# Gate, up and down products of a GEGLU feed-forward with fp32 operands in column tiles of 32, instead of three products of split operands

## The chip, the cores and the metric

The kernel runs on one core of a Trainium2 chip. The core has TensorE for matrix products (PE in the profile, its weight loads PEld), VectorE (DVE), ScalarE (ACT), GpSimd (POOL) and SyncE (SP), which issues the DMAs here. Matrix products read SBUF and write PSUM, of which the kernel uses eight banks of 128 partitions by 512 fp32 numbers. The metric is the device time of one execution in microseconds, the median over runs.

A matmul takes a stationary operand, the weights, loaded by an instruction of its own, and streams a moving operand past it. Both operands of the kernel are fp32 numbers in memory. A product can be asked for in `fp32r`, a reduced form, or in `fp32`.

## The reference

One transformer block on 2048 tokens of width 576 (D), 32 heads of 18, a feed-forward of width 4608 (F), everything in fp32:

```python
xn = _layernorm(x, axis=-1)
s = _A_ref(xn, A_wqkv, A_wo)          # softmax attention over all 2048 keys
g = _silu(_B_ref(xn, B_w_gate, B_w_up, B_w_down))
return x + s * g
# _B_ref: (gelu(x @ w_gate) * (x @ w_up)) @ w_down
```

Gelu is the tanh form.

## The kernel before

Tokens are taken in four blocks of 512 (`TB`). The kernel has four stretches.

- *Projections* (pool `pro`). For each block: layer norm, transposition of the normalized tokens by TensorE (`transposes`), a copy to SBUF with a split into a high and a low part by `split_t` (ScalarE copies into an fp32r tile, VectorE subtracts), queries and keys (`project`), values (`values_of`). The transposed tokens go to DRAM as two parts (`store_xt`, tensor `xhs`), from where `load_xd` brings them back for the feed-forward, with a GpSimd copy into the other half of the partitions.
- *Lead* (ten sections): feed-forward sections, the later ones with the maxima of the first scores between their products.
- *Attention* (128 sections): each holds a feed-forward section and a quarter of the attention of four heads over one token block.
- *Epilogue* (six sections): the rest of the feed-forward with the output projection.

A *section* (function `section`) makes one hidden tile of 128 of the 4608 hidden columns for one block: 4 blocks x 36 tiles = 144 sections. The contraction over D = 576 goes in nine chunks of 64 rows. The gate weights lie in partitions 0 to 63 and the up weights in 64 to 127, and so do two copies of the tokens, so that `gate_up` runs a gate product `pg` and an up product `pu` side by side in the two row halves of the array. Each chunk has three terms: high weights by high tokens, low by high, high by low. That is 27 pairs of matmuls of 64 x 128 weights by 512 tokens, all fp32r. The weights come by `load_gu`, one section ahead, and are split by GpSimd in `split_gu` (L106 the high part, L108 the low one).

Between these pairs stand the *specials* of the section: in the attention stretch 16 pairs, each a score product `pe` (L729) in one row half and a product `pm` for the running maximum of later scores (L698) in the other, both 64 x 128 and fp32r. `spread` deals them out evenly. ScalarE turns `pe` into exponentials (L730), VectorE reduces `pm` (L699). Every second section also multiplies exponentials by values (`acc`, L764): an unsplit fp32 product with 128 rows and 32 weight columns for each of four heads, the four in the four column groups of the array.

`activate` makes the hidden tile: Square on ScalarE (L426), VectorE (L427), tanh (L437), then VectorE once more (L440); up times gate is taken out of PSUM before that (L431, L434). `finish` splits the result into `hh` and `hl` (L106, L108) and the down weights into `dh` and `dl`.

Two hidden tiles make a *down* round (`G = 2`): eight sums of 128 tokens by 288 columns, each of 2 tiles x 3 terms, added to `Y` by VectorE (L453). In the attention stretch `half_downs` makes them with 64 rows at a time, one row half working on one sum while the other works on another, held apart by marks on ScalarE (L470). Nine of the 72 rounds are made by `down` with all 128 rows. A round's products stand behind the gate and up products of the section after its second tile.

TensorE takes its instructions in the order of the program (`manual_schedule`); the order on the other engines comes from the framework's scheduler, with some instructions kept in program order (`kept`, `no_sync`). SP issues all DMAs in one order. Tags `f`, `m` and `s` name the PSUM banks: 2, 3 and 3.

Of the kernel before, what the change touches and what calls it, by code (L numbers as in the profile page):

```python
# [17 lines left out]
P = 128  # L18
# [29 lines left out]
BANKS = {"f": 2, "m": 3, "s": 3}  # L48
EPS = 1e-5
# [20 lines left out]
def kernel(ctx: ExitStack, tc: tile.TileContext, x, wqkv, wo, w_gate, w_up, w_down, out):  # L70
# [19 lines left out]
    xhs = [dram.tile([2, D, TB], F32, name=f"xhs{b}") for b in range(NB)]  # L90
# [28 lines left out]
    def raw_tile(shape, pool=wts):  # L119
        return pool.tile(shape, F32, name="raw", tag="raw", bufs=2)  # L120

    def load_gu(t, keep=lambda i: i):

        raw = raw_tile([P, NC, P])
        for a, w in enumerate((w_gate, w_up)):
            keep(nc.sync.dma_start(raw[HR * a:HR * a + HR], w[:, t * P:(t + 1) * P].rearrange("(k p) n -> p k n", p=HR)))
        return raw, [], []

    def split_gu(w, k, keep=lambda i: i):
        hi, lo = (wts.tile([P, XG, P], F32R, name=m, bufs=5) for m in ("wh", "wl"))  # L130
        first = split(hi, lo, w[0][:, XG * k:XG * k + XG, :], keep)
        w[1].append(hi)
        w[2].append(lo)
        return first

    def load_xd(b, key=None):

        xd = [[], []]
        for c in range(0, NC, XG):
            for i in range(2):  # L140
                t = wts.tile([P, XG, TB], F32R, name=f"xd{i}_{c}")
                asked[:] = [nc.sync.dma_start(f(t)[0:HR], xhs[b][i, c * HR:(c + XG) * HR, :]
                                              .rearrange("(k p) t -> p k t", p=HR))]
                if key:
                    no_sync(asked[0], key, "keys first")
                copied[:] = [nc.gpsimd.tensor_copy(t[HR:P], t[0:HR])]
                xd[i].append(t)
        return xd
# [8 lines left out]
    with tc.tile_pool(name="pro", bufs=1) as pro, tc.tile_pool(name="pps", bufs=1, space=PSUM) as pps:  # L157
# [27 lines left out]
        def split_t(pt, k, xt):  # L185

            if k < KT:
                nc.scalar.activation(xt[0][:, k, :], pt, AF.Copy)
# [45 lines left out]
        def transposes(b, xr):  # L234
            xt = XT[b % 2]
            pts = [pps.tile([P, TB], F32, name="pt", bufs=KT + 1) for k in range(KT + 1)]
            for j in range(4):
                if b == 0 and j == 0:
                    warm(46)
                for k in range(KT + 1):  # L240
                    nc.tensor.transpose(pts[k][:, j * P:(j + 1) * P], xr[j][:, k * P:(k + 1) * P], ident)  # L241
            for k in range(KT + 1):
                split_t(pts[k], k, xt)
            return xt

        def store_xt(b, xt):
            keep = tc.keep_in_program_order if b == 0 else lambda i: i
            for i in range(2):
                keep(nc.sync.dma_start(xhs[b][i, 0:R0, :].rearrange("(k p) t -> p k t", p=P), f(xt[i])))
                keep(nc.sync.dma_start(xhs[b][i, R0:D, :], f(xt[2])[HR * i:HR * i + HR, :]))  # L250
# [96 lines left out]
        for b in range(NB):  # L347
# [29 lines left out]
            if b == 2:  # L377
                ahead = load_gu(0, tc.keep_in_program_order)
                for k in range(NG):
                    split_gu(ahead, k)  # L380
# [22 lines left out]
    def gate_up(tag):  # L403

        w, xd = FF["w"], FF["xd"]
        pg, pu = (ps.tile([P, TB], F32, name=n, tag=tag, bufs=BANKS[tag]) for n in ("pg", "pu"))
        terms = [(wp, *divmod(c, XG), xp) for c in range(NC) for wp, xp in ((0, 0), (1, 0), (0, 1))]

        def pair(i):
            wp, k, c, xp = terms[i]  # L410
            for a, o in enumerate((pg, pu)):
                rr = slice(HR * a, HR * a + HR)
                nc.tensor.matmul(o, w[1 + wp][k][rr, c, :], xd[xp][k][rr, c, :], start=(i == 0),  # L413
                                 stop=(i == len(terms) - 1))

        return [lambda i=i: pair(i) for i in range(len(terms))], pg, pu
# [6 lines left out]
    def activate(pg, pu, early):  # L423

        t1 = ffn.tile([P, TB], F32, name="t1", bufs=2)
# [10 lines left out]
        def rest(behind=None, evicted=None):  # L436
            tanh = kept(nc.scalar.activation(t1, t1, AF.Tanh, scale=GC * GS))  # L437
            if behind:
                no_sync(tanh, behind, "a mark first")
            one = kept(nc.vector.scalar_tensor_tensor(t1, t1, 1.0, t2 if early else pg, op0=ALU.add, op1=ALU.mult))  # L440
# [17 lines left out]
    DOWN = [(a, w, g) for g in range(G) for a, w in ((0, 0), (0, 1), (1, 0))]  # L458
# [4 lines left out]
    def down_product(py, hs, wd, j, c, i, rr=slice(0, P), start=False, stop=False):  # L463
        a, w, g = DOWN[i]
        return nc.tensor.matmul(py, hs[g][a][rr, j * P:(j + 1) * P], wd[w][rr, g, 288 * c:288 * c + 288],  # L465
                                start=start, stop=stop)
# [7 lines left out]
    def half_downs(b, r, hs, wd, Y):  # L474
# [9 lines left out]
        def downs_of(a, ks):  # L484
            for k in ks:
                for i in range(m):
                    def step(k=k, i=i):
# [6 lines left out]
                        one = down_product(pys[k], hs, wd, j, c, i, slice(HR * a, HR * a + HR), fresh,  # L494
                                           begun == 0 and i == m - 1)
                        if begun == 0 and i == 0 and k in seen:
                            after(one, seen[k])
# [31 lines left out]
    def load_down(r, raw):  # L529
        kept(nc.sync.dma_start(raw, w_down[r * G * P:(r + 1) * G * P, :].rearrange("(g p) n -> p g n", p=P)))  # L530
        return raw

    def section(specials=(), tag="f", raw_d=None, ahead=True):
# [17 lines left out]
        if nxt:  # L551
            for k in range(NG - 1 if ahead else 0):
                first = split_gu(nxt, k, kept)
                if k == 0 and n in ATT and n > ATT.start:
                    no_sync(first, FF["hl"], "hidden values first")
        if g == G - 1:
            FF["rawd"] = load_down(r, raw_d() if raw_d else raw_tile([P, G, D])) if ahead else FF.pop("next_d")
        for p in spread(pairs, specials):
            p()
        if nxt and ahead:  # L560
            split_gu(nxt, NG - 1, kept)
# [15 lines left out]
    def finish(pool=ffn, cut=split, bufs=1):  # L577

        n = FF["n"] - 1
        b, r = divmod(n // G, NR)  # L580
        hh = ffn.tile([P, TB], F32R, name="hh", bufs=G + 1)
        hl = ffn.tile([P, TB], F32R, name="hl", bufs=G + 1)
        first = cut(hh, hl, FF["act"])
        if n in ATT and copied:
            no_sync(first, copied.pop(), "transposed x first")
        FF["hl"] = low_part[0]
        FF["hs"].append((hh, hl))
        if n % G == G - 1:
            wd = [pool.tile([P, G, D], F32R, name=m, bufs=bufs) for m in ("dh", "dl")]
            cut(*wd, FF["rawd"])  # L590
            for h in range(2):
                once = n in ATT and n + G in ATT
                FF["down"].append((b, r, FF["hs"], wd, FF["Y"], (2 * h, 2 * h + 1), once, n + 1 + (0 if once else h)))
# [51 lines left out]
    with tc.tile_pool(name="att", bufs=1, reuse_waits="tile") as att:  # L645
# [155 lines left out]
        def lead_raw():  # L801
            t = att.tile([P, QD, TB], F32, name="pT", bufs=8)
            return t.rearrange("p a t -> p (a t)")[:, 0:G * D].rearrange("p (g d) -> p g d", g=G)

# [7 lines left out]
        for n, m in enumerate(FIRST):  # L812
            none = [lambda: None]
            lead = [lambda s=s: lead_pair(s) for s in range(slot, slot + m)]
            section((n == 2) * 5 * none + lead + (m > 0 and n != 2) * none, "s" if n == 1 else "f", lead_raw)
# [12 lines left out]
            finish(cut=split_ap)  # L828
# [28 lines left out]
    with tc.tile_pool(name="epi", bufs=1, reuse_waits="tile") as epi:  # L857
# [57 lines left out]
        def cut(hi, lo, raw):  # L915
            split_av(hi, lo, raw, kept)

# [11 lines left out]
        def next_weights(n):  # L929


            if n + 2 < ENDS:
                FF["next_gu"] = load_gu((len(FIRST) + n + 2) % (NR * G), kept)
            if n % G == 0:
                FF["next_d"] = load_down((len(FIRST) + n) // G % NR, epi.tile([P, G, D], F32, name="raw", tag="raw"))

        done = 0
        for n in range(NU * NA, ENDS):
# [23 lines left out]
            else:  # L962
                next_weights(n)
                for k in range(0 if last else NG - 1):
                    split_gu(FF["w"], k, kept)
            downs()
            run_rest()
            if first or last:
                finish(epi, cut, 2)
            else:  # L970
                for i in range(3):
# [6 lines left out]
                    if i == 0:  # L978
                        split_gu(FF["w"], NG - 1, kept)
                    prepare(done - 1 + AHEAD)  # L980
                    if i == 1:
                        finish(epi, cut, 2)
# [59 lines left out]
```

## Time and profile before

| | |
|---|---|
| time, median of 3 runs | 2548.07 us (2547.3 to 2548.31) |
| profiled execution, first to last instruction | 2545.4 us; its own device time is not listed, the runs lie 1.9 to 2.9 us above this span |
| TensorE | 2538.4 us busy (100%), 23974 matmuls |
| VectorE | 1950.4 us busy (77%) |
| ScalarE | 1555.1 us busy (61%) |
| GpSimd | 1320.7 us busy (52%) |
| HBM traffic | 126 GB/s over the span |

Busy time is a share of the span; matmuls are pipelined, so a busy TensorE is not TensorE at its peak, and how far apart matmuls start says more than how long one lasts. In the groups, "L413 PE MATMUL pg<-xd,wh" is the matmul of line 413 that writes tile `pg` from `xd` with weights `wh`; "64*128" are the rows and columns of the array that it uses; behind the bar stand busy time in us, mean ns of one, and the engine's idle time before them with what ended it. A line of the timeline has its start in us, its length, the engine and the instruction; equal neighbours are merged with a count.

### The profile page before, as it was taken

What the parts mean: (1) busy time and instruction counts of PE and PEld (TensorE: products, weight loads), DVE (VectorE), ACT (ScalarE), POOL (GpSimd) and SP (SyncE); (2) the same over time, 40 slices, a digit from 0 to 9 for tenths busy, and PEclk for the clock granted to TensorE, in tenths of its full rate; (3) what the DMA queues carried; (4) which work ended last, traced back from release to release, by engine and by line L of the source; (5) the groups of instructions that cost most, each with busy time, mean ns of one, the idle gap of its engine ahead of it and who ended that gap; (6) DMA issues with size and microseconds to landing.
All of it is one profiled execution on the core that took longest, in us unless ns stands there. A gap on an engine that the chain in (4) does not pass through costs nothing.

```text
span 2545.4 us, 63167 instructions
## 1 busy us (share of the span) xinstructions
PE 2538.4 (100%) x23974; PEld 2008.4 (79%) x23974; DVE 1950.4 (77%) x3499; ACT 1555.1 (61%) x3050; POOL 1320.7 (52%) x1447
## 2 busy tenths in 40 slices
PE   9999999999999999999999999999999999999999
PEld 8888877777777777777777787777777777787798
DVE  5316988888888888888888888888888888887277
ACT  3223366666677666676666677666676666676612
POOL 2117545555465554445565545554446555455675
PEclk9999999999999999999999999999999999999999
DMA  8876444444465444444455444444446444444483
GB/s 267 269 241 158 100 103 106 100 111 109 107 150 121 104 109 112 113 112 110 111 125 140 116 111 106 105 108 112 109 109 153 115 109 109 108 106 99 114 242 107
DMA packets 398686, 325.51 MB, mean 128 GB/s; under 512 B 117408, under 2 KB 309184, under 8 KB 398384
## 3 DMA queue, kind: packets, MB, share of 16 engines
q1 hardware_dynamic: 398384, 321.47, 49.7%
q8 instruction: 191, 3.13, 0.5%
q14 instruction: 111, 0.91, 0.1%
HBM read 266.63 MB, written 54.70 MB: 126 GB/s over the span
## 4 chain that ended last, share of the span: by engine, by line
PE 98%; ACT 1%; DVE 0%; DMA 0%; SPq 0%; issue 0%; ACTq 0%
PE pg L413 29%; PE py L465 18%; PE acc L764 18%; PE pm L698 9%; PE pe L729 9%; PE po L180 7%; PE pu L413 6%; PE po L902 2%; ACT pT L730 1%; PE pt L241 0%; SPq L665 0%; DMA xx<-in_A_x_dram 0%; DVE bs L209 0%; ACT t L426 0%; DMA KS<-qk 0%
## 5 line engine op out<-in xcount | busy, mean ns | idle before, releaser
L730 ACT ACTIVATE pT<-pe 128x512 f32<-128x512 f32 x2048 | 1153.3, 598 | 368.7 <-PE pm L698 226.3
L699 DVE TENSOR_REDUCE mx<-pm 128x1 f32<-128x512 f32 x2048 | 1249.6, 680 | 151.3 <-PE pm L698 149.0
L413 PE MATMUL pg<-xd,wh 64*128 64x512 f32 x2592 | 928.9, 390 | 0.0
L413 PE MATMUL pu<-xd,wh 64*128 64x512 f32 x2592 | 928.6, 390 | 0.0
L698 PE MATMUL pm<-KS,q 64*128 64x512 f32 x2048 | 779.0, 388 | 0.8 <-DMA KS<-qk 0.5
L729 PE MATMUL pe<-q,KS 64*128 64x512 f32 x2048 | 775.2, 387 | 0.0
L413 PEld LDWEIGHTS pg<-xd,wh 64*128 64x128 f32 x2592 | 476.5, 184 | 115.9 <-POOL wh L106 21.1
L413 PE MATMUL pg<-xd,wl 64*128 64x512 f32 x1296 | 501.6, 387 | 0.0
L413 PE MATMUL pu<-xd,wl 64*128 64x512 f32 x1296 | 501.4, 387 | 0.0
L413 PEld LDWEIGHTS pu<-xd,wh 64*128 64x128 f32 x2592 | 477.0, 184 | 2.0
L764 PE MATMUL acc<-pT,VS 128*32 128x512 f32 x4096 | 452.8, 594 | 0.0
L108 POOL TENSOR_TENSOR wl<-raw,wh 128x384 fp32r<-128x384 f32 x432 | 434.2, 1019 | 13.7
L106 POOL TENSOR_SCALAR hh<-t 128x512 fp32r<-128x512 f32 x128 | 79.1, 618 | 652.0 <-DVE t L440 637.8
L698 PEld LDWEIGHTS pm<-KS,q 64*128 64x128 f32 x2048 | 374.2, 184 | 31.1 <-DVE mx L699 4.3
L729 PEld LDWEIGHTS pe<-q,KS 64*128 64x128 f32 x2048 | 370.9, 184 | 21.9
L465 PE MATMUL py<-dh,hh 64*128 64x288 f32 (+1 forms) x2160 | 360.3, 294 | 0.3
L465 PE MATMUL py<-dl,hh 64*128 64x288 f32 (+1 forms) x2160 | 358.7, 292 | 0.0
L465 PE MATMUL py<-dh,hl 64*128 64x288 f32 (+1 forms) x2160 | 358.3, 292 | 0.0
L764 PEld LDWEIGHTS acc<-pT,VS 128*32 128x32 f32 x4096 | 127.4, 110 | 289.9 <-issue 278.0
L106 POOL TENSOR_SCALAR wh<-raw 128x384 fp32r<-128x384 f32 x432 | 217.2, 515 | 143.7 <-PE pu L413 83.4
L453 DVE TENSOR_TENSOR Y<-py,Y 128x288 f32<-128x288 f32 x544 | 227.1, 452 | 59.8 <-PE py L465 52.7
L413 PEld LDWEIGHTS pg<-xd,wl 64*128 64x128 f32 x1296 | 238.7, 184 | 32.1
(119 smaller groups left out, 3106.7 us busy)
## 6 DMA issues: line engine op xcount, KB each, us to landing
KS<-qk SPq DMA_DIRECT2D x1536, 36.0 KB
raw<-in_B_w_gate_dram SPq DMA_DIRECT2D x144, 288.0 KB
raw<-in_B_w_up_dram SPq DMA_DIRECT2D x144, 288.0 KB
raw<-in_B_w_down_dram SPq DMA_DIRECT2D x67, 576.0 KB
VS<-vs SPq DMA_DIRECT2D x128, 152.0 KB
qk<-t SPq DMA_DIRECT2D x72, 256.0 KB
q<-qk SPq DMA_DIRECT2D x384, 36.0 KB
xx<-in_A_x_dram SPq DMA_DIRECT2D x32, 288.0 KB
```

The costliest lines, as they stand in the source:

```text
L106: first = nc.gpsimd.tensor_scalar(hi, raw, 1.0, 1.0, op0=ALU.mult, op1=ALU.mult)
L108: low_part[:] = [keep(nc.gpsimd.tensor_tensor(lo, raw, f(hi), op=ALU.subtract))]
L180: nc.tensor.matmul(o, st, m, start=(i == 0), stop=(i == len(terms) - 1))
L413: nc.tensor.matmul(o, w[1 + wp][k][rr, c, :], xd[xp][k][rr, c, :], start=(i == 0), stop=(i == len(terms) - 1))
L453: one = kept(nc.vector.tensor_tensor(yy, py, yy, op=ALU.add))
L465: return nc.tensor.matmul(py, hs[g][a][rr, j * P:(j + 1) * P], wd[w][rr, g, 288 * c:288 * c + 288], start=start, stop=stop)
L698: nc.tensor.matmul(pm, QS[u, r][rr, t * P:(t + 1) * P], KS[(u * NA + c) % KB][r][rr, :], start=True, stop=True)
L699: nc.vector.tensor_reduce(MX[u][:, 2 * r + a, t, c:c + 1], pm, axis=AX.X, op=ALU.max)
L729: nc.tensor.matmul(pe, KS[(u * NA + c) % KB][r][rr, t * P:(t + 1) * P], QS[u, r][rr, :], start=True, stop=True)
L730: nc.scalar.activation(PT[u, kt][:, 2 * r + a, :], pe, AF.Exp, scale=SCALE)
L764: nc.tensor.matmul(ACC[u][32 * a:32 * a + 32, :], VS[(u * NA + c) % VB][:, v:v + 32], pt[:, a, :], start=first, stop=last, skip_group_chec ...
L902: nc.tensor.matmul(po, parts_of(b, j)[x_][:, k, :], OW[w][c][k], start=(i == 0), stop=(i == len(OUT) - 1))
```

## The change

- `gate_up` multiplies unsplit fp32 weights and tokens. Each chunk is one product per row half, made as four matmuls of 32 weight columns (`CW = 32`) into the four partition groups of the same `pg` or `pu`; gate and up alternate.
- `down_product` does the same with the hidden tile as weights: four matmuls of 32 tokens each by 288 columns. In `half_downs` they have 64 rows, in `down` 128.
- The splits of the gate, up and down weights and of the hidden tile go, with the tiles `wh`, `wl`, `hh`, `hl`, `dh`, `dl`. Weights are used from the tiles that the DMAs fill, three buffers of each kind (`gu`, `wd`).
- The transposed tokens are stored once and unsplit: `split_t` makes one more copy on ScalarE (`xf`, a single buffer), `store_xt` and `load_xd` move half the bytes, and `load_xd` makes three GpSimd copies a block where it made six.
- In the sections with early up times gate, all up to the end of the attention stretch, the last step of gelu moves from one VectorE operation to two on GpSimd.

The diff, cut to its core:

```diff
-    xhs = [dram.tile([2, D, TB], F32, name=f"xhs{b}") for b in range(NB)]
+    xhs = [dram.tile([D, TB], F32, name=f"xhs{b}") for b in range(NB)]
...
     def load_gu(t, keep=lambda i: i):
 
-        raw = raw_tile([P, NC, P])
+        t_ = wts.tile([P, NC, P], F32, name="gu", bufs=3)
         for a, w in enumerate((w_gate, w_up)):
-            keep(nc.sync.dma_start(raw[HR * a:HR * a + HR], w[:, t * P:(t + 1) * P].rearrange("(k p) n -> p k n", p=HR)))
-        return raw, [], []
-
-    def split_gu(w, k, keep=lambda i: i):
-        hi, lo = (wts.tile([P, XG, P], F32R, name=m, bufs=5) for m in ("wh", "wl"))
-        first = split(hi, lo, w[0][:, XG * k:XG * k + XG, :], keep)
...
+            keep(nc.sync.dma_start(t_[HR * a:HR * a + HR], w[:, t * P:(t + 1) * P].rearrange("(k p) n -> p k n", p=HR)))
+        return t_
...
-        def split_t(pt, k, xt):
-
+        def split_t(pt, k, xt, xf):
+
+            if k < KT:
+                nc.scalar.activation(xf[:, k, :], pt, AF.Copy)
+            else:
+                nc.scalar.activation(xf[0:HR, k, :], pt[0:HR], AF.Copy)
...
+        XF = [pro.tile([P, KT + 1, TB], F32, name="xf")] * 2
...
-        terms = [(wp, *divmod(c, XG), xp) for c in range(NC) for wp, xp in ((0, 0), (1, 0), (0, 1))]
-
-        def pair(i):
-            wp, k, c, xp = terms[i]
-            for a, o in enumerate((pg, pu)):
-                rr = slice(HR * a, HR * a + HR)
-                nc.tensor.matmul(o, w[1 + wp][k][rr, c, :], xd[xp][k][rr, c, :], start=(i == 0),
-                                 stop=(i == len(terms) - 1))
-
-        return [lambda i=i: pair(i) for i in range(len(terms))], pg, pu
+
+        def pair(c):
+            for o in range(0, P, CW):
+                for a, out_ in enumerate((pg, pu)):
+                    rr = slice(HR * a, HR * a + HR)
+                    nc.tensor.matmul(out_[o:o + CW, :], w[rr, c, o:o + CW], xd[c // XG][rr, c % XG, :], start=(c == 0),
+                                     stop=(c == NC - 1), skip_group_check=True)
+
+        return [lambda c=c: pair(c) for c in range(NC)], pg, pu
...
-            one = kept(nc.vector.scalar_tensor_tensor(t1, t1, 1.0, t2 if early else pg, op0=ALU.add, op1=ALU.mult))
-            if evicted:
-                no_sync(one, evicted, "a finished sum first")
-            if not early:
+            if early:
+                kept(nc.gpsimd.tensor_scalar(t1, t1, 1.0, 1.0, op0=ALU.add, op1=ALU.mult))
+                kept(nc.gpsimd.tensor_tensor(t1, t1, t2, op=ALU.mult))
+            else:
+                kept(nc.vector.scalar_tensor_tensor(t1, t1, 1.0, pg, op0=ALU.add, op1=ALU.mult))
                 kept(nc.vector.tensor_tensor(t1, t1, pu, op=ALU.mult))
...
-    DOWN = [(a, w, g) for g in range(G) for a, w in ((0, 0), (0, 1), (1, 0))]
+    DOWN = list(range(G))
...
     def down_product(py, hs, wd, j, c, i, rr=slice(0, P), start=False, stop=False):
-        a, w, g = DOWN[i]
-        return nc.tensor.matmul(py, hs[g][a][rr, j * P:(j + 1) * P], wd[w][rr, g, 288 * c:288 * c + 288],
-                                start=start, stop=stop)
+        for o in range(0, P, CW):
+            one = nc.tensor.matmul(py[o:o + CW, :], hs[i][rr, j * P + o:j * P + o + CW], wd[rr, i, 288 * c:288 * c + 288],
+                                   start=start, stop=stop, skip_group_check=True)
+            first = one if o == 0 else first
+        return first, one
```

More of the change, by code (lines that the diff above doesn't have):

```diff
@@ L117, in split_av, with raw_tile @@
         keep(nc.vector.tensor_tensor(lo, raw, f(hi), op=ALU.subtract))
-    def raw_tile(shape, pool=wts):
-        return pool.tile(shape, F32, name="raw", tag="raw", bufs=2)
+    def raw_tile(shape):
+        return wts.tile([P, NC, P], F32, name="gu", bufs=3).rearrange("p k n -> p (k n)")[:, 0:shape[1]]
     def load_gu(t, keep=lambda i: i):
-        raw = raw_tile([P, NC, P])
+        t_ = wts.tile([P, NC, P], F32, name="gu", bufs=3)
         for a, w in enumerate((w_gate, w_up)):
-            keep(nc.sync.dma_start(raw[HR * a:HR * a + HR], w[:, t * P:(t + 1) * P].rearrange("(k p) n -> p k n", p=HR)))
-        return raw, [], []
-    def split_gu(w, k, keep=lambda i: i):
-        hi, lo = (wts.tile([P, XG, P], F32R, name=m, bufs=5) for m in ("wh", "wl"))
-        first = split(hi, lo, w[0][:, XG * k:XG * k + XG, :], keep)
-        w[1].append(hi)
-        w[2].append(lo)
-        return first
+            keep(nc.sync.dma_start(t_[HR * a:HR * a + HR], w[:, t * P:(t + 1) * P].rearrange("(k p) n -> p k n", p=HR)))
+        return t_
     def load_xd(b, key=None):
-        xd = [[], []]
+        xd = []
         for c in range(0, NC, XG):
[L140 to L147, printed above, removed]
+            t = wts.tile([P, XG, TB], F32, name=f"xd{c}")
+            asked[:] = [nc.sync.dma_start(t[0:HR], xhs[b][c * HR:(c + XG) * HR, :].rearrange("(k p) t -> p k t", p=HR))]
+            if key:
+                no_sync(asked[0], key, "keys first")
+            copied[:] = [nc.gpsimd.tensor_copy(t[HR:P], t[0:HR])]
+            xd.append(t)
         return xd
@@ L247, in store_xt @@
             keep = tc.keep_in_program_order if b == 0 else lambda i: i
-            for i in range(2):
-                keep(nc.sync.dma_start(xhs[b][i, 0:R0, :].rearrange("(k p) t -> p k t", p=P), f(xt[i])))
-                keep(nc.sync.dma_start(xhs[b][i, R0:D, :], f(xt[2])[HR * i:HR * i + HR, :]))
+            keep(nc.sync.dma_start(xhs[b][0:R0, :].rearrange("(k p) t -> p k t", p=P), XF[b % 2][:, 0:KT, :]))
+            keep(nc.sync.dma_start(xhs[b][R0:D, :], XF[b % 2][0:HR, KT, :]))
         XT = [(pro.tile([P, KT, TB], F32R, name=f"xth{i}"), pro.tile([P, KT, TB], F32R, name=f"xtl{i}"),
                pro.tile([P, TB], F32R, name=f"xtr{i}")) for i in range(2)]
+        XF = [pro.tile([P, KT + 1, TB], F32, name="xf")] * 2
         VN = [pro.tile([P, H // 2, DH + 1], F32, name=f"vn{i}") for i in range(8)]
@@ L423, in activate @@
     def activate(pg, pu, early):
-        t1 = ffn.tile([P, TB], F32, name="t1", bufs=2)
+        t1 = ffn.tile([P, TB], F32, name="t1", bufs=G + 2)
         kept(nc.scalar.activation(t1, pg, AF.Square))
@@ L493, in step @@
                         begun = a if k < low else 1 - a
-                        one = down_product(pys[k], hs, wd, j, c, i, slice(HR * a, HR * a + HR), fresh,
+                        first, one = down_product(pys[k], hs, wd, j, c, i, slice(HR * a, HR * a + HR), fresh,
                                            begun == 0 and i == m - 1)
                         if begun == 0 and i == 0 and k in seen:
-                            after(one, seen[k])
+                            after(first, seen[k])
                         if i == m - 1:
@@ L527, in down, with load_down, section @@
                 kept(nc.sync.dma_start(ys[b * TB + j * P:b * TB + (j + 1) * P, :], Y[:, j]))
[L529 to L533, printed above, removed]
+    def load_down(r):
+        wd = wts.tile([P, G, D], F32, name="wd", bufs=3)
+        kept(nc.sync.dma_start(wd, w_down[r * G * P:(r + 1) * G * P, :].rearrange("(g p) n -> p g n", p=P)))
+        return wd
+    def section(specials=(), tag="f", ahead=True):
         n = FF["n"]
@@ L551, in section @@
         if nxt:
[L552 to L555, printed above, removed]
+            pass
         if g == G - 1:
-            FF["rawd"] = load_down(r, raw_d() if raw_d else raw_tile([P, G, D])) if ahead else FF.pop("next_d")
+            FF["rawd"] = load_down(r) if ahead else FF.pop("next_d")
         for p in spread(pairs, specials):
             p()
-        if nxt and ahead:
-            split_gu(nxt, NG - 1, kept)
         FF["w"] = nxt
@@ L575, in downs, with finish @@
             down(*FF["down"].pop(0)[:-1])
-    def finish(pool=ffn, cut=split, bufs=1):
+    def finish():
         n = FF["n"] - 1
         b, r = divmod(n // G, NR)
[L581 to L587, printed above, removed]
+        FF["hs"].append(FF["act"])
         if n % G == G - 1:
-            wd = [pool.tile([P, G, D], F32R, name=m, bufs=bufs) for m in ("dh", "dl")]
-            cut(*wd, FF["rawd"])
             for h in range(2):
                 once = n in ATT and n + G in ATT
-                FF["down"].append((b, r, FF["hs"], wd, FF["Y"], (2 * h, 2 * h + 1), once, n + 1 + (0 if once else h)))
+                FF["down"].append((b, r, FF["hs"], FF["rawd"], FF["Y"], (2 * h, 2 * h + 1), once, n + 1 + (0 if once else h)))
     def load_numbers(num, rb, g, toks):
@@ L814 @@
             lead = [lambda s=s: lead_pair(s) for s in range(slot, slot + m)]
-            section((n == 2) * 5 * none + lead + (m > 0 and n != 2) * none, "s" if n == 1 else "f", lead_raw)
+            section((n == 2) * 5 * none + lead + (m > 0 and n != 2) * none, "s" if n == 1 else "f")
             if slot + m >= NS > slot:
@@ L934, in next_weights @@
             if n % G == 0:
-                FF["next_d"] = load_down((len(FIRST) + n) // G % NR, epi.tile([P, G, D], F32, name="raw", tag="raw"))
+                FF["next_d"] = load_down((len(FIRST) + n) // G % NR)
         done = 0
```

20 lines of the change are left out of this document (5 added, 15 removed).

## The prediction

> **What bounds the kernel now.** I read the page from its head to the chain, then the groups by shape, then single instructions in the timeline.
>
> ```profile
> span 2545.4 us, 63167 instructions
> ...
> PE 2538.4 (100%) x23974; PEld 2008.4 (79%) x23974; DVE 1950.4 (77%) x3499; ACT 1555.1 (61%) x3050; POOL 1320.7 (52%) x1447
> ...
> PEclk9999999999999999999999999999999999999999
> ...
> PE 98%; ACT 1%; DVE 0%; DMA 0%; SPq 0%; issue 0%; ACTq 0%
> PE pg L413 29%; PE py L465 18%; PE acc L764 18%; PE pm L698 9%; PE pe L729 9%; PE po L180 7%; PE pu L413 6%; PE po L902 2%; ACT pT L730 1%; PE pt L241 0%; SPq L665 0%; DMA xx<-in_A_x_dram 0%; DVE bs L209 0%; ACT t L426 0%; DMA KS<-qk 0%
> ```
>
> TensorE has matmuls in flight all the time at full clock, and the chain that ended last is 98% its own. The next engine, VectorE, has 595 us to spare. So the change is worth what it does to the time the array needs; what it frees elsewhere counts only where TensorE now waits, and it hardly waits. The spans add up to 2545.4 us here and the runs read 2547.3 to 2548.31, so I add 2.7 us for what lies around the span.
>
> The counts that the terms need, from the groups by shape:
>
> ```profile
> L413 PE MATMUL pg<-xd,wh 64*128 64x512 f32 x2592 | 928.9, 390 | 0.0
> L413 PE MATMUL pg<-xd,wl 64*128 64x512 f32 x1296 | 501.6, 387 | 0.0
> L764 PE MATMUL acc<-pT,VS 128*32 128x512 f32 x4096 | 452.8, 594 | 0.0
> L465 PE MATMUL py<-dh,hh 64*128 64x288 f32 x2016 | 315.8, 293 | 0.2
> L465 PE MATMUL py<-dh,hh 128*128 128x288 f32 x144 | 44.5, 309 | 0.1
> ```
>
> Gate and up make 3888 steps of one pg and one pu matmul side by side in the two row halves (2592+1296): 1296 chunks of three terms. The down products make 504 sums in half rows (2016 = 504 sums x 2 hidden tiles x 2 halves) and 72 in full rows (144/2). The third row is the model for the new work: `acc` is an unsplit fp32 product with 32 weight columns. The program has 2048 of them and the trace 4096 matmuls, so each is two instructions, two passes.
>
> **What a step costs, before and after.** Timeline of TensorE inside a section, then inside a down sum:
>
> ```profile
> 1200.11 0.39 PE L413 MATMUL pg<-xd,wh 64*128 64x512 f32 x1
> ...
> 1202.83 0.39 PE L413 MATMUL pg<-xd,wh 64*128 64x512 f32 x1
> ```
>
> ```profile
> 1209.83 0.30 PE L465 MATMUL py<-dh,hl 64*128 64x288 f32 x2
> ...
> 1211.16 0.29 PE L465 MATMUL py<-dh,hh 64*128 64x288 f32 x2
> ```
>
> Between the first two lie 12 steps (gate and score pairs alike): 2.72/12 = 0.2267 us each. Between the second two lie 10: 0.133 us each. The fp32 passes show best in the weight loads, which come in fours, one per group of 32 columns, at the start of each pass:
>
> ```profile
> 1228.27 0.13 PEld L764 LDWEIGHTS acc<-pT,VS 128*32 128x32 f32 x4 [0.30 <-issue]
> ...
> 1229.98 0.13 PEld L764 LDWEIGHTS acc<-pT,VS 128*32 128x32 f32 x4 [0.30 <-issue]
> 1230.95 0.18 PEld L413 LDWEIGHTS pg<-xd,wh 64*128 64x128 f32 x1 [0.84 <-POOL hh L106]
> ```
>
> Four passes in 1.71 us: 0.4275 us for one pass of four column groups at once, and a product needs two. So a 512-column fp32 product over all 128 columns takes 0.855 us where three fp32r terms take 3 x 0.2267 = 0.680.
>
> *Gate and up.* 1296 chunks, each 8 products now (4 column groups x 2 row halves). I take it that all eight run together, as four do in `acc` and two row halves do in the pg/pu rows: 1296 x (0.855-0.680) = **+227 us**.
>
> *Down.* A pass over 288 columns is 0.4275 x 288/512 = 0.2405 us. A sum is 2 hidden tiles x 2 passes = 0.962 us for both halves together, where 6 steps were 0.798: +0.164 x 576 sums = **+94 us**.
>
> *Crossings between tile shapes.* The score products stay at 64 rows x 128 columns; gate, up and half-row down products become 64x32. Sections interleave 9 chunks with the score pairs, so nearly every chunk is now alone between other shapes. The built order of the changed kernel has 2476 changes of shape against 159, 2317 more, and 1203 visits to 64x32. What a change costs:
>
> ```profile
> 493.40 0.39 PE L413 MATMUL pu<-xd,wh 64*128 64x512 f32 x1
> 493.72 1.50 PE L764 MATMUL acc<-pT,VS 128*32 128x512 f32 x12
> ```
>
> Into `acc`: the pu matmul has its 0.227 us until 493.63, acc starts at 493.72: 0.09 lost. Out of it: the load at 1229.98 goes with the last but one pass, so the last one starts at 1230.41, its last column group 0.02 later, and is through at 1230.86; the gate starts at 1230.95: 0.09 to 0.10. I take 0.096: 2317 x 0.096 = **+222 us**. The trace has no change between 64x128 and 64x32 (both halve the rows): the lower bound is 0 (2935 us in all), the upper the 0.09 with an unhidden load of 0.11 on top, 0.20 (about 3400). I take the rows that are nearest, changes of column count with the row count changing too. The Trainium skill, "TensorEngine Tiling (Array Packing)", section Key Properties, says that changing the mode, not just the tile, drains the array; by it the 0.096 holds for this pair too, and without it the sum would be 222 lower.
>
> *Skew.*
> ```profile
> L764 PEld LDWEIGHTS acc<-pT,VS 128*32 128x32 f32 x4096 | 127.4, 110 | 289.9 <-issue 278.0 <-DVE mx L699 10.2 <-ACT pT L730 1.1
> ```
>
> Four loads take 0.13 us and one 0.11, so tiles start 0.0067 us apart; the eighth starts 0.047 behind the first and each visit ends that much later: 1203 x 0.047 = **+56 us** (none if the drain hides it, bounded by that).
>
> *Splits.* They leave GpSimd and the DMAs of xd halve:
>
> ```profile
> L108 POOL TENSOR_TENSOR wl<-raw,wh 128x384 fp32r<-128x384 f32 x432 | 434.2, 1019 | 13.7
> L106 POOL TENSOR_SCALAR wh<-raw 128x384 fp32r<-128x384 f32 x432 | 217.2, 515 | 143.7 <-PE pu L413 83.4 <-DMA raw<-in_B_w_up_dram 55.6 <-PE pm L698 3.4
> L108 POOL TENSOR_TENSOR hl<-t,hh 128x512 fp32r<-128x512 f32 x128 | 164.7, 1287 | 10.7
> L106 POOL TENSOR_SCALAR hh<-t 128x512 fp32r<-128x512 f32 x128 | 79.1, 618 | 652.0 <-DVE t L440 637.8 <-PE py L465 13.8
> L440 DVE SCALAR_TENSOR_TENSOR t<-t,t 128x512 f32<-128x512 f32 x138 | 97.3, 705 | 16.1 <-ACT t L437 2.0
> ```
>
> The removed 651 us of wh and wl lie beside a busy TensorE: **0**. In 138 sections gelu's end moves from VectorE (0.7 us) to two GpSimd operations of the kinds of hh and hl (0.6 + 1.3 us), which is what the two splits of t took there before; the hidden tile is used by the down sums behind the next section's gate, 27 + 16 steps of 0.2267 or 9.7 us later in the old order: **0**. If that cover were gone, 138 x 1.2 us = 166 us would be the bound. The early `rest` had a VectorE order behind an eviction, which falls away: nothing queues there. Weight tiles have three buffers, a load being issued a section ahead, so SP meets no new wait.
>
> *Projections.* ScalarE copies each transposed block once more:
>
> ```profile
> L188 ACT ACTIVATE xth<-pt 128x512 fp32r<-128x512 f32 x16 | 8.3, 604 | 2.6 <-PE pt L241 2.6
> 46.66 0.42 SPq L249 DMA_DIRECT2D xhs<-xth  x1
> 47.63 0.77 ACT L300 ACTIVATE vn<-po 128x288 f32<-128x288 f32 x2
> ```
>
> For block 0 the five copies stand on the path: 5 x 0.6 = 3 us. `xf` has one buffer, so block 1's copy waits until block 0's store, issued near 46.7, has landed, and the value evictions queue behind it on ScalarE; three PSUM banks, 14 matmuls of 0.133 us each, cover 5.6 us of it. Later blocks store long before. I take **+10** (3 to 25).
>
> Sum: 227 + 94 + 222 + 56 + 10 = 609. 2545.4 + 609 + 2.7 = **3157 us**.
>
> **The rivals.**
>
> *Row halves follow each other within a column group.* In the built program the two passes of a product stand one behind the other, product after product.
>
> ```profile
> 493.72 0.16 PEld L764 LDWEIGHTS acc<-pT,VS 128*32 128x32 f32 x8 [0.35 <-DVE mx L699]
> 494.17 0.13 PEld L764 LDWEIGHTS acc<-pT,VS 128*32 128x32 f32 x4 [0.30 <-issue]
> ```
>
> A run of `acc` begins with eight loads in 0.16 us, both passes of four products, and goes on in fours: the array takes four column groups together, out of that order. It shows nothing on two row halves of one column group in such a stream. If a column group takes its queue in order, the up product's first pass runs with the gate product's second; in a long run nothing is lost, but a visit alone takes three passes: 1203 x 0.4275 = +514, 3671 us. For it: no row shows the opposite. Against: fp32r row halves run together freely.
>
> *Row halves exclude each other in column tiles.* Gate and half-row sums double: 1296 x 0.855 + 504 x 0.962 = +1593, 4750 us. Against: 64-row pairs overlap fully in the pg/pu rows.
>
> *Strict order.* Matmuls start in program order only, so a product's second pass blocks the next product's first: 9 passes for a chunk (3.85 us) and about 3.85 for a sum. +2.99 x 1296 + 2.89 x 504 + 0.96 x 72 = +5400, 8560 us. Against: four of `acc`'s loads start within 0.13 us, pass after pass. The Trainium skill, "TensorE: Matmul & The Clock Gate", section "The mechanism", has this rule: matmuls keep strict order in start and end. By it the time would be those 8560 us; the trace's fours speak against it.
>
> *Faster: the pass is not 0.4275 here.* `acc` streams four different moving tiles; gate and up stream the same chunk of x into all four column groups. If the four streams, not the passes, set 0.4275, a pass could fall to 0.2267 (512 columns) and 0.133 (288): gate 1296 x (0.453-0.680) = -294, down 576 x (0.532-0.798) = -153, with crossings, skew and projections as above: 2389 us. It decides below 0.271 us a pass of 512: all gate and down passes together are 1296 x 2 + 576 x 4 x 288/512 = 3888 such lengths, and the terms they replace, 881 + 460 us, leave 1053 after the 288 us of crossings, skew and projections. Against: 0.4275 is nearly twice 0.2267, a round ratio that fits two trips per pass better than a port; no row has four groups with one stream.
>
> **How the numbers follow.** The forecast has 0.72, with a range of its own of 2935 to 3400 from the crossing's two bounds. In-order column groups 0.13, exclusive halves 0.05, strict order 0.02, the faster pass 0.05; 0.03 for what I have not named. The range, 2930 to 3680, holds the forecast's nearly whole and most of the in-order case. A measurement of this kernel tells 0.2%, some 5 us, from no change: faster 0.06, same 0.01, slower 0.93.
>
> **What would show it.** Right: TensorE still over 95% of the chain; gate and up loads in eights with 0.43 us between passes; a lone chunk some 1.0 us from its first load to the next score pair and a score pair some 0.32 from the chunk behind it; GpSimd below 20% busy; sections of 19 to 21 us instead of 16.3, which is a 128th of this stretch, from the first attention section to the last:
>
> ```profile
> 325.00:2417.00 2092.00, 2091.82 (x20920) 1617.81 (x20912) 1676.24 (x3011) 1423.97 (x2807) 1112.52 (x1220) 1.00 0.47 113
> ```
>
> Wrong: three steps of 0.43 per lone chunk (in-order column groups), four (exclusive halves), steps near 0.23 (the faster rival), or long waits of TensorE for t (the gelu cover gone). The weakest steps are the price of a crossing and whether eight tiles run at once.

## The result, and the profile after

The changed kernel takes 3302.89 us (median of four runs, 3302.0 to 3304.23) beside 2547.69 us for the kernel before (2547.11 to 2548.31): a ratio of 1.2963, 95% interval 1.2945 to 1.2982. It is 755 us slower. The forecast was 3157 us: the sign and the range hold, the value is 146 us low. The execution that the profile shows took 3302.4 us, 1.8 us above its span.

The page of the changed kernel: head, chain, and the groups that answer to those shown of before. Gate and up are line 406 now, down 459, `pm` 682, `pe` 713, `acc` 748, gelu's GpSimd end 434.

```profile
span 3300.6 us, 109460 instructions
...
PE 3288.1 (100%) x47734; PEld 1276.3 (39%) x47734; DVE 1949.4 (59%) x3352; ACT 1532.7 (46%) x3046; POOL 412.0 (12%) x448
...
PE 98%; DMA 1%; DVE 0%; issue 0%; ACT 0%; POOL 0%; SPq 0%; DVEq 0%
PE pg L406 37%; PE py L459 17%; PE acc L748 14%; PE pe L713 11%; PE pm L682 10%; PE po L172 4%; PE pu L406 2%; PE po L882 2%; DMA gu<-in_A_wqkv_dram 0%; DMA wd<-in_B_w_down_dram 0%; DMA qk<-t 0%; DMA xhs<-xf 0%; PE pt L237 0%; DMA xx<-in_A_x_dram 0%; POOL ql L109 0%
...
L406 PE MATMUL pg<-xd,gu 64*32 64x512 f32 x10368 | 1384.1, 600 | 0.2 <-issue 0.2
...
L713 PE MATMUL pe<-q,KS 64*128 64x512 f32 x2048 | 769.9, 452 | 0.0
...
L748 PE MATMUL acc<-pT,VS 128*32 128x512 f32 x4096 | 452.8, 594 | 0.0
...
L434 POOL TENSOR_SCALAR t<-t 128x512 f32<-128x512 f32 x138 | 85.6, 620 | 2054.3 <-ACT t L430 1973.9
```

The bound has not moved: TensorE holds 98% of the chain as before, the other engines have more idle time than they had (GpSimd 52% to 12%). The recorded waits of its matmuls add up to 9 us in this kernel and to 3 us before. So all but a few of the 755 us are time that the array itself takes. One row is strange. The score product `pe` was not touched, and its 2048 matmuls had this row before:

```profile
L729 PE MATMUL pe<-q,KS 64*128 64x512 f32 x2048 | 775.2, 387 | 0.0
```

Its mean went from 387 to 452 ns. That is the trail to the missing 146 us. I divided both spans at the first gate product and at the first and last `acc`. Projections went from 196.2 to 204.0 us, the lead from 128.1 to 167.7, attention from 2092.7 to 2785.1, the epilogue from 128.5 to 143.9. So 692 of the 755 us lie in the attention stretch, 21.8 us a section (2785.1/128) where it was 16.3. This is TensorE there, one chunk of gate and up with the two score pairs behind it, up to the next chunk:

```profile
1709.10 0.61 PE L406 MATMUL pg<-xd,gu 64*32 64x512 f32 x1
...
1709.14 0.61 PE L406 MATMUL pu<-xd,gu 64*32 64x512 f32 x1
1709.55 0.59 PE L406 MATMUL pg<-xd,gu 64*32 64x512 f32 x1
...
1710.12 0.49 PE L682 MATMUL pm<-KS,q 64*128 64x512 f32 x1
1710.12 0.72 PE L713 MATMUL pe<-q,KS 64*128 64x512 f32 x2
1710.45 0.39 PE L682 MATMUL pm<-KS,q 64*128 64x512 f32 x1
1710.78 0.61 PE L406 MATMUL pg<-xd,gu 64*32 64x512 f32 x1
```

All eight tiles of the first pass start between 1709.10 and 1709.14, the second pass follows 0.45 us later, the score pair 0.57 after that, the second score pair 0.33 later and the next chunk 0.33 after it. The period is 1.68 us. The forecast had the same order of events; it had 0.43, 0.57, 0.23 and 0.32. Two gaps are too long, and both are the second start after a change of tile shape. The weight loads of the same stretch show why:

```profile
1710.12 0.18 PEld L682 LDWEIGHTS pm<-KS,q 64*128 64x128 f32 x1 [0.84 <-DVE mx L683]
1710.12 0.29 PEld L713 LDWEIGHTS pe<-q,KS 64*128 64x128 f32 x2
1710.23 0.19 PEld L682 LDWEIGHTS pm<-KS,q 64*128 64x128 f32 x1
1710.78 0.10 PEld L406 LDWEIGHTS pg<-xd,gu 64*32 64x32 f32 x1 [0.36 <-issue]
```

At 1710.12 the first score pair is recorded as starting in the same instant as its own loads: no load has gone ahead across the change. The load of the second pair (1710.23) does run beside a matmul. So the first product after a change is in the array for some 0.1 us longer (0.49 where the others have 0.39), and what follows it is late by as much. The bracket of the first line has the 0.84 us in which no load ran and names VectorE as what came last before this one; but VectorE is not what held these products: 1057 of the 1064 score pairs behind a gate and up pass start 0.565 or 0.566 us after that pass, whatever VectorE did, and the view of the matmuls' waits has no line for `mx`. The same delay stands in the trace of the kernel before too, just behind a row that the prediction quotes (its gate load at 1230.95, after a run of `acc`):

```profile
1230.96 0.50 PE L413 MATMUL pg<-xd,wh 64*128 64x512 f32 x1
...
1231.29 0.39 PE L729 MATMUL pe<-q,KS 64*128 64x512 f32 x1
...
1231.53 0.39 PE L413 MATMUL pg<-xd,wl 64*128 64x512 f32 x1
```

The step from 1231.29 to 1231.53 is near the usual 0.23. The one from 1230.96 to 1231.29 is 0.33: the drain had been read off, the load behind it had not. That the 0.1 us is the load is a reading so far; the tiles of 64 columns below test it.

### The profile page after: what moved, and what is told of

The parts are those of the page before. It is cut to its first block, busy times and chain, and to the rows that moved or that the text cites. A ratio compares the mean times of both kernels' runs of the same rounds, so it can differ in the third digit from the quotient of the medians.

```text
span 3300.6 us, 109460 instructions
## 1 busy us (share of the span) xinstructions
PE 3288.1 (100%) x47734; PEld 1276.3 (39%) x47734; DVE 1949.4 (59%) x3352; ACT 1532.7 (46%) x3046; POOL 412.0 (12%) x448
## 4 chain that ended last, share of the span: by engine, by line
PE 98%; DMA 1%; DVE 0%; issue 0%; ACT 0%; POOL 0%; SPq 0%; DVEq 0%
PE pg L406 37%; PE py L459 17%; PE acc L748 14%; PE pe L713 11%; PE pm L682 10%; PE po L172 4%; PE pu L406 2%; PE po L882 2%; DMA gu<-in_A_wqkv_dram 0%; DMA wd<-in_B_w_down_dram 0%; DMA qk<-t 0%; DMA xhs<-xf 0%; PE pt L237 0%; DMA xx<-in_A_x_dram 0%; POOL ql L109 0%
## 5 line engine op out<-in xcount | busy, mean ns | idle before, releaser
L406 PE MATMUL pg<-xd,gu 64*32 64x512 f32 x10368 | 1384.1, 600 | 0.2 <-issue 0.2
L406 PE MATMUL pu<-xd,gu 64*32 64x512 f32 x10368 | 1384.1, 600 | 0.0
L459 PE MATMUL py<-wd,t 64*32 64x288 f32 (+1 forms) x17280 | 579.1, 403 | 1.9 <-issue 1.9
L459 PEld LDWEIGHTS py<-wd,t 64*32 64x32 f32 (+1 forms) x17280 | 354.2, 107 | 241.7 <-issue 52.5
L406 PEld LDWEIGHTS pg<-xd,gu 64*32 64x32 f32 x10368 | 237.8, 105 | 450.8 <-issue 450.3
L406 PEld LDWEIGHTS pu<-xd,gu 64*32 64x32 f32 x10368 | 237.6, 105 | 0.8 <-issue 0.5
L420 DVE SCALAR_TENSOR_TENSOR t<-t,pg 128x512 f32<-128x512 f32 x144 | 97.8, 679 | 177.6 <-ACT t L419 177.6
L419 ACT ACTIVATE t<-pg 128x512 f32<-128x512 f32 x144 | 86.0, 597 | 207.2 <-PE pu L406 172.9
L435 POOL TENSOR_TENSOR t<-t,t 128x512 f32<-128x512 f32 x138 | 177.2, 1284 | 11.5
L427 DVE TENSOR_TENSOR t<-t,pg 128x512 f32<-128x512 f32 x138 | 94.3, 684 | 23.0 <-ACT t L424 23.0
```

The costliest lines, as they stand in the source:

```text
L406: nc.tensor.matmul(out_[o:o + CW, :], w[rr, c, o:o + CW], xd[c // XG][rr, c % XG, :], start=(c == 0), stop=(c == NC - 1), skip_group_check ...
L420: kept(nc.vector.scalar_tensor_tensor(t1, t1, 1.0 / GC, pg, op0=ALU.add, op1=ALU.mult))
L427: nc.vector.tensor_tensor(t2, t2, pg, op=ALU.mult)
L435: kept(nc.gpsimd.tensor_tensor(t1, t1, t2, op=ALU.mult))
L459: one = nc.tensor.matmul(py[o:o + CW, :], hs[i][rr, j * P + o:j * P + o + CW], wd[rr, i, 288 * c:288 * c + 288], start=start, stop=stop, s ...
```

## The experiments

The theory after the result was this: passes cost what the forecast gave them, and a visit to the 64x32 shape costs more than forecast, because the first product on each side of it waits for its own load. Rivals: the fp32 passes themselves are slower in column tiles or in pairs of row halves; evictions or gelu's new end hold TensorE; the down sums lose. Where an expectation speaks of a bank wait, that is TensorE waiting for a PSUM bank that VectorE or ScalarE has not yet read.

**Wide tiles: no change of shape at all**

```diff
-CW = 32
+CW = 128
```

Every fp32 product is one matmul of 128 columns, the shape of the score products.

> The changed kernel with 128 weight columns in one matmul instead of four of 32: unsplit fp32 operands as before, but gate, up and half-row down products have the shape of the score products again (64 rows by 128 columns), so the 1203 visits to another shape are gone. Theory (shape changes): a pass of both row halves still takes 0.43 us, a chunk 0.86, and each visit that falls away saves 0.37 us (0.10 into it, 0.025 on its first pass, 0.137 out of it, 0.108 on the first score pair behind it, by the changed kernel's timeline): 3303 - 1203 x 0.37 = about 2858 us, 2830 to 2890. Rival (the four column tiles are what gives fp32 its rate, with wide ones the loads of 128 columns or the passes do not overlap): passes longer than 0.43 us, 3300 us or more.

Measured: 2888.82 us (2887.16 to 2890.49), ratio 1.134 (1.1324 to 1.1357) to before, at the upper edge of the theory's range and far from the rival's. The same chunk and two score pairs:

```profile
1512.27 0.59 PE L406 MATMUL pg<-xd,gu 64*128 64x512 f32 x1
...
1512.71 0.59 PE L406 MATMUL pg<-xd,gu 64*128 64x512 f32 x1
...
1513.60 0.59 PE L406 MATMUL pg<-xd,gu 64*128 64x512 f32 x1
...
1516.26 0.59 PE L406 MATMUL pg<-xd,gu 64*128 64x512 f32 x1
```

The three periods from 1512.27 to 1516.26 are 1.33 us each where the changed kernel has 1.68; one pass still takes 0.43 to 0.44. So unsplit fp32 costs the same in wide tiles as in column tiles, and the two halves of the loss come apart: operands +341 us (2888.82 less 2547.55, the kernel before in the runs beside this one), tiles +414 us (3302.89 less 2888.82), or 0.344 us for each of 1203 visits.

**Gelu's end back on VectorE**

```diff
-            if early:
-                kept(nc.gpsimd.tensor_scalar(t1, t1, 1.0, 1.0, op0=ALU.add, op1=ALU.mult))
-                kept(nc.gpsimd.tensor_tensor(t1, t1, t2, op=ALU.mult))
-            else:
-                kept(nc.vector.scalar_tensor_tensor(t1, t1, 1.0, pg, op0=ALU.add, op1=ALU.mult))
+            one = kept(nc.vector.scalar_tensor_tensor(t1, t1, 1.0, t2 if early else pg, op0=ALU.add, op1=ALU.mult))
+            if evicted:
+                no_sync(one, evicted, "a finished sum first")
+            if not early:
                 kept(nc.vector.tensor_tensor(t1, t1, pu, op=ALU.mult))
```

> The changed kernel with the end of gelu back on VectorE as one operation (and its order behind an eviction back), nothing else. Theory (TensorE bounds, the hidden tile is due a section later): no difference, 3298 to 3308 us. Rival (GpSimd's 1.9 us where VectorE took 0.7 delays the down sums): up to 138 x 1.2 = 166 us less, 3140 us.

Measured: 3303.02 us (3300.42 to 3306.02), the changed kernel's time. Its page shows that the work moved and that TensorE is as busy as it was (3288.1 us in the changed kernel):

```profile
PE 3287.0 (100%) x47734; PEld 1276.3 (39%) x47734; DVE 2035.8 (62%) x3490; ACT 1532.7 (46%) x3046; POOL 149.2 (5%) x172
```

**Chunks in twos and in threes: fewer visits**

```diff
-        for p in spread(pairs, specials):
+        groups = [lambda i=i: [p() for p in pairs[i:i + 2]] for i in range(0, len(pairs), 2)]
+        for p in spread(groups, specials):
```

The second kernel has 3 in place of 2. Visits fall from 1203 to 681 and 414; the score pairs stand in longer runs between them.

> The changed kernel with the nine chunks of a section dealt out in groups of two (2, 2, 2, 2, 1) between the score pairs: 681 visits to the 64x32 shape instead of 1203, the same matmuls. Theory (shape changes): 522 x 0.37 = 193 us less, about 3110 us. Rival (the longer runs of score pairs wait for PSUM banks instead: three banks, VectorE at 0.68 us a tile, three to four pairs in a run): the gain is given back at some 0.3 us a run, 3250 to 3300 us, with idle TensorE in front of the fourth pair of a run.

> The changed kernel with the chunks in groups of three: 414 visits instead of 1203, score pairs in runs of five and six. Theory (shape changes alone): 789 x 0.37 = 292 us less, about 3011 us. Rival (banks): each pair behind the third waits for VectorE, 0.68 us a pair less the 0.23 it takes, two to three pairs a run, 1 us a run, 384 runs: +380 us, about 3390 us. A time between the two measures the bank wait.

Measured: 3257.65 us (3256.32 to 3258.42) in twos, and 3478.65 us (3477.34 to 3481.12) in threes, slower than the change itself. Saving visits alone would have given 2889 + 681 x 0.344 = 3123 and 3031 us. The trace of the first, a run of four score pairs:

```profile
1507.53 0.50 PE L714 MATMUL pe<-q,KS 64*128 64x512 f32 x1
...
1507.87 0.62 PE L714 MATMUL pe<-q,KS 64*128 64x512 f32 x2
1508.11 0.39 PE L683 MATMUL pm<-KS,q 64*128 64x512 f32 x1
1508.85 0.49 PE L683 MATMUL pm<-KS,q 64*128 64x512 f32 x1 [0.35 <-DVE mx L684]
```

and of the second:

```profile
1510.69 0.39 PE L714 MATMUL pe<-q,KS 64*128 64x512 f32 x1
1511.33 0.50 PE L714 MATMUL pe<-q,KS 64*128 64x512 f32 x1 [0.26 <-ACT pT L715]
...
1511.99 0.50 PE L714 MATMUL pe<-q,KS 64*128 64x512 f32 x1
1512.42 0.61 PE L406 MATMUL pg<-xd,gu 64*32 64x512 f32 x1
```

Three banks serve each kind of score product, and VectorE needs 0.69 us on average for the maximum of one, ScalarE 0.60 for the exponentials. The first three pairs find free banks and go 0.34 and 0.24 apart; the fourth stands 0.74 behind the third and has again a matmul of 0.49: its loads are unhidden, as after a change of shape. In threes most runs are five or six pairs long, and the later pairs wait for both engines: 0.64 and 0.66 us apart in the lines above. The view of waits of the kernel in twos has a line that the changed kernel's has not:

```profile
PE pm L683 <- DVE mx L684: 46.2, 129, 0.6
```

The rival expectation (bank waits) was right in size for the twos; for the threes it was 90 us low. In twos the unrounded starts (of a pair, the later of its two products) place the whole difference. The 123 fourth pairs cost 64 us more than a usual step. In 121 of the 492 runs of three the third pair waits as well, which makes 49 us. The chunks behind these runs come 25 us later than elsewhere. That is 138 us, where the time lies 135 above 3123. In threes the third to sixth pairs and the chunks behind them cost 435 of the 448 us above 3031. So 0.344 us a visit and the bank waits together account for both kernels within 13 us. By themselves the two times do not measure the price of a visit; they say that lone chunks also pace the score pairs. The next kernel goes at the parts of the price.

**Tiles of 64 columns: other loads, other skew, same visits**

```diff
-CW = 32
+CW = 64
```

> The changed kernel with two products of 64 weight columns in place of four of 32 (64x64 tiles in gate, up and half-row down products). The order of the sections and the number of visits (1203) stay; four tiles run together in place of eight. Theory (a visit costs the drain on both sides, the skew of the tiles, and the weight loads of the first pass after each change, which nothing can pull ahead): skew 3 x 0.0067 = 0.02 in place of 0.047, -32 us; the first pass of a visit waits for loads of 64 columns, about 0.053 in place of 0.025, +33 us: 3290 to 3315, and the first pass of a visit lasts some 0.48 us in place of 0.454, the others 0.429. The second score pair after a visit stays 0.335 behind the first. If the load that shows does not go with the columns, 3271. If passes of wider tiles cost more, 3400 and up. If row halves exclude each other in tiles of 64 columns, about 4700.

Measured: 3297.16 us (3295.07 to 3299.01). The period of the timeline:

```profile
1709.12 0.64 PE L406 MATMUL pg<-xd,gu 64*64 64x512 f32 x1
...
1709.60 0.59 PE L406 MATMUL pg<-xd,gu 64*64 64x512 f32 x1
...
1710.14 0.49 PE L682 MATMUL pm<-KS,q 64*128 64x512 f32 x1
...
1710.80 0.64 PE L406 MATMUL pg<-xd,gu 64*64 64x512 f32 x1
```

Again 1.68 us, but put together otherwise: the first pass takes 0.48 (0.45 with 32 columns), the way out 0.54 (0.57). With the unrounded starts, the first pass is 0.051 above the 0.429 of a pass where it was 0.024, and the way out 0.110 above it where it was 0.137: 0.027 less for four tiles fewer, which is 4 x 0.0067. Load and skew are two things, the first goes with the columns and the second with the number of tiles, and here they cancel to within 6 us, as the theory had it. What is lost at the first product goes with its columns: 0.024 for 32, 0.051 for 64 and, behind the first score pair, 0.108 for 128. The records of the loads themselves last longer, 0.10, 0.13 and 0.18 us. The Trainium skill, "TensorE: Matmul & The Clock Gate", section "LDWEIGHTS (loading the stationary operand)", has a load time that goes with the columns alone, P/1.2 ns; by it I estimate 27, 53 and 107 ns, and the three delays are within 3 ns of that. The run also answers a rival that was not named: it has 28726 matmuls where the changed kernel has 47734, so the loss does not go with the number of instructions.

**Gate and up alone, down alone**

In the first, gate and up are as in the changed kernel and the down products as before, with split operands in three terms; in the second it is the other way round. Both end gelu on VectorE. The core of the two edits against the changed kernel, first gate and up alone, then down alone:

```diff
-        FF["hs"].append(FF["act"])
+        hh = ffn.tile([P, TB], F32R, name="hh", bufs=G + 1)
+        hl = ffn.tile([P, TB], F32R, name="hl", bufs=G + 1)
+        cut(hh, hl, FF["act"])
+        FF["hs"].append((hh, hl))
```

```diff
-        def pair(c):
-            for o in range(0, P, CW):
...
+        def pair(i):
+            wp, k, c, xp = terms[i]
```

> Gate and up products as in the changed kernel; down products as before, with the split operands hh, hl, dh, dl in three terms; the splits of these stay on GpSimd, and gelu ends on VectorE. Its order has 1206 visits to 64x32. Theory, with the price of a visit as the changed kernel's trace has it (0.099 + 0.025 + 0.137 + 0.108 = 0.369 us): 2548 + 227 + 1206 x 0.369 + 8 = 3228, so 3210 to 3245. With the price of the forecast (0.239) 3071. If the extra time beyond the forecast came from the down products (their loads, or waits on marks), 3070 to 3120.

> Down products as in the changed kernel; gate and up as before, in three split terms with 64x128 tiles. Its order has 63 visits to 64x32 and 16 to 128x32 beyond those of acc. Theory: 2548 + 94 + 79 x 0.369 = 2671, so 2655 to 2680. If the half-row sums lose by themselves (rows exclude each other, waits for banks or marks), over 2700. If a visit cost several times 0.369, as a run's end behind many loads might, 63 visits could add 60 more: 2730.

Measured: 3202.94 us (3202.54 to 3203.58) for gate and up alone, ratio 1.2573 (1.2555 to 1.2592), and 2667.43 us (2666.39 to 2668.42) for down alone, ratio 1.0471 (1.0455 to 1.0487). Down alone lands in its range: +120 us; if the passes have the forecast's 94, the 79 visits have the rest, 0.33 us each. Gate and up alone add 655 us; less the forecast's 227 for the passes and 8 for the projections, 420 us remain, 0.348 us for each of 1206 visits. That is the 0.344 of the wide comparison, and 7 us under the range that I had made with 0.369. So nothing hides in the down products: the two parts add up to 775 us where both together cost 755, and both together have 66 visits fewer than the parts: 1206 + 79, less 1203 to 64x32 and 16 to 128x32 (66 x 0.344 = 23).

None of these kernels is faster than the kernel before. The nearest, down alone, is 4.7% behind it.

## Why the prediction was right in sign and 146 us low

- *Bound.* Right: TensorE still has 98% of the chain at full clock, and what was freed elsewhere bought nothing.
- *Gate, up and down passes, +227 and +94, projections +10.* Right: the wide kernel has these three terms alone and measured +341 against 331. A pass is 0.429 us rather than 0.4275, which over the 3888 lengths of 512 is 6 us.
- *Projections.* Right in place: the copy of block 1 into `xf` waits for the store of block 0, as the forecast said. The stretch grew by 7.8 us.

```profile
55.62 0.60 ACT L180 ACTIVATE xf<-pt 128x512 f32<-128x512 f32 x1 [2.67 <-DMA xhs<-xf]
```

- *Splits and gelu at nothing.* Right: the kernel with gelu's end on VectorE has the same time, and GpSimd sat at 12% (forecast below 20%). That the splits were worth nothing was not tested by itself; it rests on the sums above, which leave nothing for them.
- *Skew, 0.047 a visit.* Right: the tiles of 64 columns, four fewer, took 0.027 less.
- *Crossings between tile shapes, 0.096 each.* Wrong, and the only wrong step. Crossings and skew were forecast at 278 us and measured at 414. The drain is right: from the last pass to the score pair 0.137 above a pass (0.143 forecast with the skew), from the last score pair to the chunk 0.099 above a step (0.096). What was left out is the load of the first product after each change. The prediction named it, as the upper bound "0.09 with an unhidden load of 0.11 on top", and chose the rows of `acc`, reading only the gap up to the first start; the load shows one start later. (That 0.11 is the recorded length of a load of 32 columns in the prediction's rows; that a load of 128 columns came out at 0.108 is chance.) In the changed kernel, from the unrounded starts: 861 second score pairs stand 0.335 behind the first where 0.227 is usual (+93 us), 326 lone score pairs have the chunk 0.432 behind them where 0.326 is usual (+35), and 1203 first passes last 0.024 longer (+29): 157 us. The operands' 10 above forecast, these 157, and drains and skew 21 below the forecast's 278 are the 146. (By their rows the drains and the skew come to 272 us: 1064 x 0.137, 60 x 0.137 behind down sums and 1187 x 0.099. Some 15 of them are not in the comparison with the wide kernel, whose period of 1.33 us is itself 0.02 above two passes and two steps.) The row of `pe` says it in one number: 2048 x (452 - 387) ns = 133 us beside the 93 + 35.
- *Rivals.* In-order column groups would have put three passes into a lone chunk, exclusive row halves and strict order more; in the trace 2580 of the 2592 passes of gate and up have eight tiles whose starts lie within 0.05 us, two passes to a chunk, and from the second one to the score pair it is 0.57 us. The faster pass fell too: 0.429 us with one moving stream for four column groups. The Trainium skill's rule of strict order ("TensorE: Matmul & The Clock Gate", section "The mechanism") does not hold for this stream: the two passes of a product stand one behind the other in the program, yet all eight first passes start before any second one. Its page "TensorEngine Tiling (Array Packing)", section Key Properties, that a change of mode drains the array, agrees with the 0.09 to 0.10 us on each side here; it gives no price.
- *What was to show it.* Loads in eights with 0.43 us between passes, 1.02 us from a chunk to the next score pair (1709.10 to 1710.12), 0.33 from the score pair to the chunk: as forecast. Sections of 19 to 21 us: 21.8. The list had nothing on the gap between two score pairs, which is where the error stood.

## What to carry to other kernels

A visit to another tile shape has four prices: a drain on the way in, a drain on the way out, the skew of its tiles, and on each side the weight load of the first product, which was never pulled ahead across the change here. In this kernel that was 0.34 us for work of 0.86 us, and 414 of the 755 us lost. Before mixing shapes in a finely interleaved stream, count the visits in the built order and read two starts past a change, not one; and if work is gathered to save visits, check that the PSUM banks of what stands between still turn over.

## What the runs showed of the hardware that was not expected

- An unsplit fp32 product of 512 columns takes two passes of 0.43 us in tiles of 32, 64 and 128 columns alike, so column tiles bring it nothing by themselves: 2888.8 us wide against 3302.9 in 32s and 3297.2 in 64s.
- A change from unsplit fp32 to fp32r at the same tile shape costs next to nothing (1.33 us a period in the wide kernel where passes and steps alone make 1.31). It is the shape that drains.
- After a wait for a PSUM bank the loads are unhidden as well (0.49 us matmuls behind the waits in the kernels of twos and threes), so such a wait costs about a tenth of a microsecond more than its own length: the chunk behind a fourth pair that waited starts 0.43 us after it where 0.33 is usual.
